# A fused attention and gMLP kernel: its order of all steps made anew, k's maxima in three steps, part of the layer-norm statistics on ScalarE

## The chip, the cores and the metric

The kernel runs on one core of one Trainium2 chip. Its engines run side by side, each with a queue of its own that it works off in order: TensorE does matrix products into PSUM, VectorE, ScalarE and GpSimd do elementwise work, and SyncE issues the transfers between the chip's memory and SBUF. The profile calls them PE (PEld for the loading of its weights), DVE, ACT, POOL and SP. The metric is the device time in microseconds (us), the median of several runs.

## The reference

For 8 batches and 8 heads with 576 positions of 64 channels, q is normalised by a softmax over its channels, k by a softmax over the positions; each head's 64x64 matrix `kv` and then its output come from products with these. The heads side by side are the 512 channels of `x`, which goes through a gated MLP:

```python
q_s = exp(q - max(q, axis=-1));  q_s /= sum(q_s, axis=-1) + 1e-09
k_s = exp(k - max(k, axis=2));   k_s /= sum(k_s, axis=2) + 1e-09
kv = einsum('bhsd,bhse->bhde', k_s, v)
x = einsum('bhsd,bhde->bhse', q_s, kv)      # heads side by side: (8, 576, 512)
h = gelu_tanh(x @ w_in)                     # (8, 576, 1024)
u, v = h[..., :512], h[..., 512:]
v_n = (v - mean(v)) / sqrt(var(v) + 1e-06) * g_ln      # over the 512 channels
v_s = einsum('ts,bsd->btd', w_sg, v_n) + b_sg[None, :, None]
out = x + (u * v_s) @ w_out
```

## The kernel before

**Sets and halves.** A batch is called a set, b = 0 to 7. q, k and v of a set come in two halves of four heads. SBUF has two buffers for each half-set of q, k, v, so SyncE (`Y`) fetches ahead.

**Precision.** fp32 values go through TensorE in a shorter fp32 form (fp32r): a value is split into a high part (a copy, which rounds) and a low part (value minus high part), and a product is made of three matmuls, high x high, low x high and high x low. Names that end in `_h` and `_l` (`wi`, `ws`, `wo` for w_in, w_sg, w_out; `x`; `vnh`, `vnl`; `gh`, `ulow`) are such parts. w_in and w_out arrive as 64-bit numbers and are turned into fp32 on the chip, a slice of 128 columns at a time (8 slices of w_in): `wi_a` scales the upper word on ScalarE, `wi_b`, `wi_c`, `wi_d` are a shift and two bit operations on VectorE that write tile `ot_i`, `wi_h` copies the high part on ScalarE, and `wi_l` subtracts for the low part, on GpSimd or, where the step says V, on VectorE. `wo_a` to `wo_l` do this for w_out with tile `ot_o`.

**The stages of a set.** k: `k_max` takes the maxima over positions (three VectorE instructions on tile `km`, 512, 256 and 256 wide), `kt_mm` transposes on TensorE, `k_top` finishes the maxima (`kt`), `kb_mm` spreads them over the partitions, `k_sub` and `k_exp` follow. q: `q_max` (tile `qm`), `q_swapm`, `q_top` and `q_sub`, `q_exp`, then `q_sum` (`qd`), `q_swapd`, `q_inv`, `q_mul` for the division and `q_turn` for the transposes. `kv_mm`, `kv_inv`, `kv_scale` give kv (tile `kvt`), `x_mm` gives x in four tiles, and `x_high`, `x_low` split it. Then `hv_mm` makes a 128-position tile of v (four per set, and a fifth for the two 64-position remainders of two sets, 36 in all), `hv_gelu` its gelu on ScalarE, `hv_stat` its mean and variance on VectorE with the two batch-norm instructions and one that adds 1e-06 (`ve`), `hv_pow` the power -1/2 on GpSimd (`rs`), `hv_norm`, `hv_high`, `hv_low` the normalised tile and its parts; `tail_high`, `tail_low`, `tail_again` do this for the remainders. `hu_mm` and `hu_gelu` give u, `sg_mm` the spatial product with w_sg, `gate`, `gate_high`, `gate_low` the gating, `out_mm`, `out_add`, `out_rest`, `out_store` the end. The last tile of set 7 is added, completed and stored in two halves (`last_mm`, `last_add`, `last_rest`, `last_store`).

**PSUM.** Three pairs of banks (`ps2`) go round for x, u, the spatial and the output products; two single banks (`ps1`) go round for k's transposes, kv and `hv_mm`. A new product waits until the bank that it is given has been read.

**What sets the order.** The string `PLAN` lists 1160 steps. They are issued one after the other as listed; the wrapper `InOrder` (its inner function `issue`, line 142) ties each instruction of VectorE, ScalarE, GpSimd and SyncE to the one issued before it on the same engine, and `mm` (line 330) keeps TensorE in program order. So the order of the steps in `PLAN` is the order of every engine's queue, and the position of a step against those of other engines sets nothing by itself. Line 142 therefore stands for all elementwise work in the profile, and tile names tell the work apart. A letter behind a step (`wi_l 1 V`) chooses its engine.

## Time and profile before

| what | value |
|---|---|
| median of 3 runs | 533.68 us (532.89 to 534.45) |
| the profiled execution: time, span on the core | 533.9 us, 532.0 us |
| busy in the span: PE, PEld | 484.2 us (91%), 444.3 us (84%) |
| busy in the span: DVE, ACT, POOL | 378.7 us (71%), 249.5 us (47%), 126.1 us (24%) |
| matmuls | 3824 |
| bytes read, written in the chip's memory | 38.83 MB, 9.44 MB |
| granted TensorE clock | 1.000 |

The span runs from the first to the last instruction of one profiled execution. Busy time is the time in which an engine had an instruction running; the profile's rows give an instruction's start and duration, or a group's busy time with its mean in ns, then the idle time just ahead of the group with what ended it. The span in 40 slices of 13.3 us shows PE nearly idle in the first four slices and full in nearly all others, DVE nearly full in the first ten.

### The profile page before, as it was taken

The page shows a single profiled execution, that of the slowest core. Times are in us where ns is not written, and L with a number is a line of the kernel's source. Part 1 is how long each engine was busy: PE and PEld are TensorE (multiplying, and loading weights), DVE is VectorE, ACT ScalarE, POOL GpSimd, SP SyncE. Part 2 cuts the span into 40 slices and gives each one's busy share as a digit, 9 for nine tenths or more (in the row PEclk, how much of TensorE's full clock was granted, in tenths as well). Part 3 has the DMA queues.
Part 4 walks back from the last instruction along what each step waited for, and adds up shares of the span by engine and source line. Part 5 has one row for each costly group of instructions (what it writes and reads, how often), then busy time and mean ns, then how long its engine had stood idle before and what let it go on. Part 6 is the DMA issues. An engine that isn't in the chain of part 4 may idle for free.

```text
span 532.0 us, 9264 instructions
## 1 busy us (share of the span) xinstructions
PE 484.2 (91%) x3824; PEld 444.3 (84%) x3824; DVE 378.7 (71%) x646; ACT 249.5 (47%) x425; POOL 126.1 (24%) x104
## 2 busy tenths in 40 slices
PE   0151999999999999999999999999999999999997
PEld 0040878998998988999999988999989988999997
DVE  8999899999879788876757887966264467243114
ACT  4474784658475355762564355751064134131110
POOL 0334403341332003251211322540111102012211
PEclk9999999999999999999999999999999999999999
...
GB/s 322 369 388 96 17 217 81 1 46 121 168 90 38 253 91 2 44 101 68 130 39 101 111 123 90 1 101 123 67 1 1 68 23 0 1 1 68 23 1 90
DMA packets 19054, 48.87 MB, mean 92 GB/s; under 512 B 1602, under 2 KB 8132, under 8 KB 19012
## 3 DMA queue, kind: packets, MB, share of 16 engines
...
HBM read 38.83 MB, written 9.44 MB: 91 GB/s over the span
## 4 chain that ended last, share of the span: by engine, by line
PE 74%; DVE 17%; issue 3%; DMA 2%; ACT 2%; POOL 1%; SPq 0%; POOLq 0%; DVEq 0%; ACTq 0%
PE ps L330 74%; DVE km L142 2%; DVE ot_i L142 2%; DMA qq<-q 1%; DVE qm L142 1%; DVE qd L142 1%; DVE kk L142 1%; DVE v L142 1%; POOL qq L142 1%; DMA kk<-k 1%; DVE qq L142 1%; DVE s L142 1%; DVE x_l L142 1%; DVE wi_l L142 1%; DVE ulow L142 1%
## 5 line engine op out<-in xcount | busy, mean ns | idle before, releaser
L142 POOL TENSOR_TENSOR rs<-ve,half 128x1 f32<-128x1 f32 x36 | 31.0, 860 | 157.1 <-DVE ve L142 152.1
L142 DVE TENSOR_TENSOR u<-ps,u 128x576 f32<-128x576 f32 x32 | 24.0, 750 | 52.0 <-PE ps L330 52.0
L330 PE MATMUL ps<-ulow,wo_h 128*128 128x288 f32 x256 | 55.7, 296 | 1.2 <-DVE ulow L142 1.2
L330 PE MATMUL ps<-gh,wo_h 128*128 128x288 f32 x256 | 56.1, 298 | 0.5 <-ACT gh L142 0.5
L330 PE MATMUL ps<-ws_h,vnh 128*128 128x288 f32 x256 | 55.8, 299 | 0.0
L330 PE MATMUL ps<-gh,wo_l 128*128 128x288 f32 x256 | 55.3, 294 | 0.0
L330 PE MATMUL ps<-ws_l,vnh 128*128 128x288 f32 x256 | 54.8, 295 | 0.0
L330 PE MATMUL ps<-ws_h,vnl 128*128 128x288 f32 x256 | 54.8, 295 | 0.0
L142 ACT ACT_TABLE_LOAD x38 | 48.8, 1283 | 8.0 <-PE ps L330 5.1
L142 ACT ACTIVATE v<-ps 128x512 f32<-128x512 f32 x36 | 21.5, 598 | 63.8 <-PE ps L330 62.3
L142 ACT CAST gh<-u 128x576 fp32r<-128x576 f32 x32 | 21.5, 671 | 57.5 <-DVE u L142 57.3
L142 DVE TENSOR_TENSOR o<-ps,x_h 128x576 f32<-128x576 f32 (+1 forms) x33 | 24.2, 734 | 31.8 <-PE ps L330 31.8
L142 POOL TENSOR_TENSOR qq<-qq,qd 128x576 f32<-128x576 f32 x22 | 28.2, 1295 | 68.6 <-DVE qd L142 46.2
L330 PEld LDWEIGHTS ps<-gh,wo_h 128*128 128x128 f32 x256 | 41.4, 188 | 1.9 <-ACT gh L142 0.8
L142 POOL TENSOR_TENSOR ulow<-u,gh 128x576 fp32r<-128x576 f32 x16 | 23.8, 1487 | 80.7 <-ACT gh L142 62.9
L330 PEld LDWEIGHTS ps<-ulow,wo_h 128*128 128x128 f32 x256 | 41.2, 188 | 2.0 <-DVE ulow L142 1.9
L330 PEld LDWEIGHTS ps<-ws_h,vnh 128*128 128x128 f32 x256 | 41.3, 189 | 0.4
L330 PE MATMUL ps<-wi_h,x_h 128*128 128x512 f32 x144 | 40.7, 404 | 1.0 <-DVE kk L142 1.0
L330 PEld LDWEIGHTS ps<-ws_h,vnl 128*128 128x128 f32 x256 | 41.3, 188 | 0.0
L330 PEld LDWEIGHTS ps<-ws_l,vnh 128*128 128x128 f32 x256 | 41.3, 188 | 0.0
L330 PEld LDWEIGHTS ps<-gh,wo_l 128*128 128x128 f32 x256 | 41.2, 188 | 0.0
L330 PE MATMUL ps<-x_h,wi_h 128*128 128x288 f32 x256 | 40.8, 303 | 0.0
...
## 6 DMA issues: line engine op xcount, KB each, us to landing
vv<-v SPq DMA_DIRECT2D x16, 650.0 KB, 6.1
...
qq<-q SPq DMA_DIRECT2D x16, 576.0 KB, 3.8
...
```

The lines of the kernel that those rows point to most:

```text
L142: ins = op(*args, **kw)
L330: tc.keep_in_program_order(nc.tensor.matmul(*args, **kw))
```

## The change

`PLAN` is replaced as a whole: 1217 steps in another order. Three things beside the order differ.

- `k_max` becomes three steps, `k_ma`, `k_mb`, `k_mc`, one instruction each, the same three instructions as before; other steps may stand between them.
- For 25 of the 36 tiles of v the mean and variance come from ScalarE: `hv_gelu … A` also writes the sum of its output (`sm`), the new step `hv_sq` scales it to minus the mean (`nm`) and squares the tile with that bias into a scratch tile `sq`, with the sum in `sv`; `hv_stat … A` is then one VectorE instruction on a 128x1 tile, and `hv_norm` adds `nm` in place of subtracting the mean.
- Engine letters differ: of the eight `wi_l` six run on GpSimd and two on VectorE (before two and six), of the five `ws_l` three run on VectorE (four before), `gate_low` is on GpSimd 11 times (16), `q_sub` on VectorE 10 times (8), `out_rest` on VectorE 19 times (20), and the first half's `last_rest` is on GpSimd.

Counted over the program, VectorE has 593 instructions in place of 641, ScalarE 369 in place of 331 with 26 table loads among them in place of 38, GpSimd 102 in place of 103, TensorE as many as before. SyncE's queue begins with slices 2 and 0 of w_in, the identity and slice 3 of w_in; q and k come behind them.

```diff
 PLAN = """
-load_q 0 1, load_q 0 0, load_k 0 1, load_k 0 0, load_eye, load_w_in 1, load_w_in 7, load_w_in 0, load_w_in 2, q_max 0 1, load_v 0 1, load_v 0 0
...
+load_w_in 2, wi_a 2, wi_b 2, wi_c 2, load_w_in 0, load_eye, load_w_in 3, load_q 0 1, load_k 0 0, load_w_in 1, load_q 0 0, load_k 0 1, load_b
+load_w_in 7, wi_a 0, wi_d 2, load_w_sg 0, wi_b 0, wi_c 0, wi_d 0, load_w_sg 1, load_w_in 4, wi_h 2, wi_a 3, load_v 0 0, load_v 0 1, load_w_sg 3
...
 """
...
@@ -200,6 +204,8 @@
     qq_s = slots("qq", 2, [P, 2, 18, 32])
     km_s = slots("km", 2, [P, 512])
     kt_s = slots("kt", 2, [P, 2])
+    sq = sb("sq", [P, DV])
+    sm_s, nm_s, sv_s = (slots(n, 6, [P, 1]) for n in ("sm", "nm", "sv"))
     qm_s, qs_s, qd_s, qe_s = (slots(n, 2, [P, 36]) for n in ("qm", "qs", "qd", "qe"))
     kr_s = slots("kr", 2, [P, 2])
     kvt_s, qt_s = slots("kvt", 2, [P, 2, D]), slots("qt", 4, [P, S])
@@ -339,12 +345,18 @@
     def load_v(b, h):
         Y.dma_start(out=vv_s(b, h, at=h), in_=v[b, h])
 
-    def k_max(b, h, E=V):
-
-        kk, m = kk_s(b, h, at=h), km_s(b, h, at=2 * b + h)
-        E.tensor_tensor(out=m, in0=kk[:, 0:2].rearrange("p t c -> p (t c)"), in1=kk[:, 2:4].rearrange("p t c -> p (t c)"), op=ALU.max)
-        E.tensor_tensor(out=m[:, 0:256], in0=m[:, 0:256], in1=m[:, 256:512], op=ALU.max)
-        E.tensor_tensor(out=m[:, 0:256], in0=m[:, 0:256], in1=kk[:, 4], op=ALU.max)
+    def k_ma(b, h):
+
+        kk = kk_s(b, h, at=h)
+        V.tensor_tensor(out=km_s(b, h, at=2 * b + h), in0=kk[:, 0:2].rearrange("p t c -> p (t c)"), in1=kk[:, 2:4].rearrange("p t c -> p (t c)"), op=ALU.max)
+
+    def k_mb(b, h):
+        m = km_s(b, h)
+        V.tensor_tensor(out=m[:, 0:256], in0=m[:, 0:256], in1=m[:, 256:512], op=ALU.max)
+
+    def k_mc(b, h):
+        m = km_s(b, h)
+        V.tensor_tensor(out=m[:, 0:256], in0=m[:, 0:256], in1=kk_s(b, h)[:, 4], op=ALU.max)
 
     def columns(ps):
         return ps[:, 0:256].rearrange("p (a n) -> p a n", a=2)
@@ -486,14 +498,26 @@
                 mm(ph, lhs(b)[:, c, col:col + P], rhs[:, c, DV:2 * DV], start=m == 0, stop=m == 11)
                 m += 1
 
-    def hv_gelu(b, i):
-        A.activation(v_s(b, i), st["hv", b, i], AF.Gelu_apprx_tanh)
-
-    def hv_stat(b, i):
-        s6, mv = s6_s(b, i), mv_s(b, i)
-        V.bn_stats(out=s6, in_=v_s(b, i))
-        V.bn_aggr(out=mv, in_=s6)
-        V.tensor_scalar(out=ve_s(b, i), in0=mv[:, 1:2], scalar1=1e-6, scalar2=None, op0=ALU.add)
+    def hv_gelu(b, i, E=V):
+        if E is A:
+            sm_s.take(b, i), nm_s.take(b, i), sv_s.take(b, i)
+            A.activation(v_s(b, i), st["hv", b, i], AF.Gelu_apprx_tanh, accum_out=sm_s(b, i))
+        else:
+            A.activation(v_s(b, i), st["hv", b, i], AF.Gelu_apprx_tanh)
+
+    def hv_sq(b, i):
+
+        A.mul(nm_s(b, i), sm_s(b, i), -1.0 / DV)
+        A.activation(sq, v_s(b, i), AF.Square, bias=nm_s(b, i), accum_out=sv_s(b, i))
+
+    def hv_stat(b, i, E=V):
+        if E is A:
+            V.tensor_scalar(out=ve_s(b, i), in0=sv_s(b, i), scalar1=1.0 / DV, scalar2=1e-6, op0=ALU.mult, op1=ALU.add)
+        else:
+            s6, mv = s6_s(b, i), mv_s(b, i)
+            V.bn_stats(out=s6, in_=v_s(b, i))
+            V.bn_aggr(out=mv, in_=s6)
+            V.tensor_scalar(out=ve_s(b, i), in0=mv[:, 1:2], scalar1=1e-6, scalar2=None, op0=ALU.add)
 
     def hv_pow(b, i):
         G.tensor_tensor(out=rs_s(b, i), in0=ve_s(b, i), in1=half, op=ALU.pow)
@@ -501,7 +525,8 @@
     def hv_norm(b, i):
 
         t = v_s(b, i)
-        V.scalar_tensor_tensor(out=t, in0=t, scalar=mv_s(b, i)[:, 0:1], in1=g_bc, op0=ALU.subtract, op1=ALU.mult)
+        mean, op = (nm_s(b, i), ALU.add) if (b, i) in nm_s.turn else (mv_s(b, i)[:, 0:1], ALU.subtract)
+        V.scalar_tensor_tensor(out=t, in0=t, scalar=mean, in1=g_bc, op0=op, op1=ALU.mult)
 
     def hv_high(b, i):
         A.activation(vn_hl()[0][:, i], v_s(b, i), AF.Copy, scale=rs_s(b, i))
```

Three places of the engines' queues follow. The first is VectorE from the scaling of set 0's second kv (`kvt0_1`) through the last of set 0's four `x_l` or as far as eleven rows reach; `ot_i` and `wi_l` are the conversion of w_in, `km1`, `qm1` the maxima of set 1. Before:

```order
L142 TENSOR_TENSOR kvt0_1_329<-ps1_1_77,kr0_1_317 128x128
L142 TENSOR_REDUCE qm1_1_331<-qq1_1_221 128x36
L142 TENSOR_TENSOR x_l0_340<-ps2_1_74,x_h0_325 128x576
L142 TENSOR_TENSOR qm1_0_323<-qm1_0_323,qs1_0_333 128x36
L142 SCALAR_TENSOR_TENSOR ot_i_4_273<-raw_wo_h_85,ot_i_4_273 128x512
L142 TENSOR_TENSOR km1_0_350<-kk1_0_256 128x512
L142 TENSOR_TENSOR km1_0_350<-km1_0_350 128x256
L142 TENSOR_TENSOR km1_0_350<-km1_0_350,kk1_0_256 128x256
L142 TENSOR_TENSOR qm1_1_331<-qm1_1_331,qs1_1_342 128x36
L142 TENSOR_TENSOR wi_l_62<-ot_i_4_273,wi_h_61 128x4x128
L142 TENSOR_TENSOR wi_l_62<-ot_i_2_175,wi_h_61 128x4x128
```

And now:

```order
L146 TENSOR_TENSOR kvt0_1_322<-ps1_1_78,kr0_1_317 128x128
L146 TENSOR_TENSOR x_l0_329<-ps2_0_74,x_h0_315 128x576
L146 TENSOR_REDUCE qm1_0_333<-qq1_0_270 128x36
L146 TENSOR_TENSOR x_l0_329<-ps2_1_75,x_h0_315 128x576
L146 SCALAR_TENSOR_TENSOR ot_i_6_264<-raw_wo_l_87,ot_i_6_264 128x512
L146 SCALAR_TENSOR_TENSOR ot_i_7_175<-raw_wo_l_87,ot_i_7_175 128x512
L146 TENSOR_TENSOR qm1_0_333<-qm1_0_333,qs1_0_349 128x36
L146 TENSOR_TENSOR km1_0_285<-km1_0_285,kk1_0_246 128x256
L146 TENSOR_TENSOR km1_1_359<-kk1_1_312 128x512
L146 TENSOR_REDUCE qm1_1_365<-qq1_1_310 128x36
L146 TENSOR_TENSOR x_l0_329<-ps2_0_74,x_h0_315 128x576
L146 TENSOR_TENSOR x_l0_329<-ps2_2_76,x_h0_315 128x576
```

Before, one `x_l` stands in this stretch, and the other three come behind it; now all four stand in it, and the two `wi_l` are gone from it.

The second place is GpSimd's queue from its first piece of work, with `qq` the products of q and `ws_2` the low parts of the bias. Before:

```order
L142 TENSOR_TENSOR qq0_0_93<-qq0_0_93,qd0_0_165 128x576
L142 TENSOR_TENSOR qq0_1_91<-qq0_1_91,qd0_1_152 128x576 x2
L142 TENSOR_TENSOR ws_2_66<-vb_0_89,ws_2_66 1x320
L142 TENSOR_TENSOR ws_2_66<-vb_1_90,ws_2_66 1x320
L142 TENSOR_TENSOR wi_l_62<-ot_i_3_206,wi_h_61 128x4x128
L142 TENSOR_TENSOR wi_l_62<-ot_i_7_267,wi_h_61 128x4x128
L142 TENSOR_TENSOR ws_l_64<-ghws_3_150,ws_h_63 128x640
L142 TENSOR_TENSOR qq1_0_191<-qq1_0_191,qm1_0_323 128x1152
L142 TENSOR_TENSOR qq1_1_221<-qq1_1_221,qm1_1_331 128x1152
L142 TENSOR_TENSOR qq1_0_191<-qq1_0_191,qd1_0_381 128x576 x2
```

And now:

```order
L146 TENSOR_TENSOR wi_l_62<-ot_i_2_93,wi_h_61 128x4x128
L146 TENSOR_TENSOR wi_l_62<-ot_i_3_124,wi_h_61 128x4x128
L146 TENSOR_TENSOR wi_l_62<-ot_i_1_152,wi_h_61 128x4x128
L146 TENSOR_TENSOR ws_l_64<-ghws_0_115,ws_h_63 128x640
L146 TENSOR_TENSOR qq0_0_105<-qq0_0_105,qd0_0_190 128x576 x2
L146 TENSOR_TENSOR qq0_1_100<-qq0_1_100,qd0_1_210 128x576 x2
L146 TENSOR_TENSOR wi_l_62<-ot_i_4_198,wi_h_61 128x4x128
L146 TENSOR_TENSOR wi_l_62<-ot_i_5_266,wi_h_61 128x4x128
L146 TENSOR_TENSOR qq1_0_270<-qq1_0_270,qm1_0_333 128x1152
L146 TENSOR_TENSOR qq1_1_310<-qq1_1_310,qm1_1_365 128x1152
```

Three `wi_l` now open the queue and two more stand ahead of set 1's q; before there were two in this stretch, behind q of set 0 and the bias.

The third place is ScalarE around the first statistics of v, with `u0` and `v0` the gelus of set 0 and `kk1` the exponentials of k of set 1. Before:

```order
L142 ACTIVATE v0_3_475<-ps1_1_77 128x512
L142 COPY qe1_1_480<-qd1_1_445 32x36 x4
L142 ACTIVATE u0_1_500<-ps2_2_75 128x576
L142 ACT_TABLE_LOAD
L142 ACTIVATE kk1_0_256<-kk1_0_256 128x1280
L142 ACT_TABLE_LOAD
L142 ACTIVATE v0_1_534<-ps1_1_77 128x512
L142 ACT_TABLE_LOAD
L142 ACTIVATE kk1_1_313<-kk1_1_313 128x1280
```

And now:

```order
L146 ACTIVATE u0_2_523<-ps2_2_76 128x576
L146 ACTIVATE u0_1_525<-ps2_1_75 128x576
L146 ACTIVATE v0_3_527,sm0_3_528<-ps1_0_77 128x512
L146 COPY qe1_1_530<-qd1_1_476 32x36 x4
L146 ACTIVATE nm0_3_535<-sm0_3_528 128x1
L146 ACTIVATE sq_73,sv0_3_537<-v0_3_527,nm0_3_535 128x512
L146 ACT_TABLE_LOAD
L146 ACTIVATE kk1_1_312<-kk1_1_312 128x1280
L146 ACT_TABLE_LOAD
L146 ACTIVATE v0_1_590,sm0_1_591<-ps1_0_77 128x512
```

The gelu of tile 3 now also writes `sm`, and the scaling to `nm` and the square with its sum stand between that gelu and k's exponentials.

More of the change, by code (lines that the diff above doesn't have):

```diff
@@ new lines @@
+x_high 0 1, q_max 1 0, x_mm 0 1, load_w_out 3, wi_l 5, ws_h 2, load_v 1 0, x_low 0 1, q_swapm 1 0, wi_c 6, wi_d 7, wi_h 7, q_top 1 0, k_mc 1 0
+k_ma 1 1, kt_mm 1 0, x_high 0 2, x_high 0 3, q_max 1 1, q_sub 1 0, q_swapm 1 1, wo_a 1, x_low 0 3, x_low 0 2, hu_mm 0 1, k_mb 1 1, k_top 1 0, k_mc 1 1
+q_top 1 1, q_exp 1 0, wo_a 0, ws_h 1, kb_mm 1 0, kt_mm 1 1, hu_mm 0 2, wi_l 7 V, wi_d 6, wi_h 6, k_sub 1 0, q_sub 1 1, k_top 1 1, k_exp 1 0, q_sum 1 0
+wi_l 6, kb_mm 1 1, hv_mm 0 3, q_exp 1 1, k_sub 1 1, b_l, wo_a 3, q_swapd 1 0, wo_a 2, q_sum 1 1, kv_mm 1 0, hu_mm 0 0, wo_b 1, hu_gelu 0 2
```

189 lines of the change are left out of this document (94 added, 95 removed).

## The prediction

> **What bounds the kernel now.** I read the split of the span by stage first, cutting it where the PE timeline changes character: 4 us (first data on DVE), 54 us (first dense matmul), 97 us (first spatial matmul), 168 us, 515 us. Columns: stage, its length, then busy us (and instructions) of PE, PEld, DVE, ACT, POOL.
>
> ```profile
> 4.00:54.00 50.00, 12.90 (x121) 7.78 (x121) 48.10 (x76) 27.73 (x57) 15.32 (x10) 1.00 0.83 296
> 54.00:97.00 43.00, 41.72 (x308) 35.30 (x309) 39.87 (x79) 30.13 (x53) 11.07 (x11) 1.00 0.30 97
> 97.00:168.00 71.00, 69.50 (x567) 66.52 (x566) 63.12 (x100) 44.85 (x78) 23.22 (x17) 1.00 0.24 80
> 168.00:515.00 347.00, 347.00 (x2736) 322.07 (x2737) 218.30 (x378) 144.83 (x238) 74.89 (x61) 1.00 0.18 64
> ```
>
> From 168 to 515 us PE never pauses, so there nothing but the number of matmuls counts, and the change keeps that number. All that can be won lies ahead of 168 us. In the first 50 us DVE is busy for 48.1 us and PE for 12.9; from 54 to 97 us DVE still has only 3.1 us free. Next, PE's waits, for 54 to 168 us and then for 168 us to the end:
>
> ```profile
> PE ps L330 <- DVE ulow L142: 1.0, 2, 0.7
> PE ps L330 <- DVE kk L142: 1.0, 1, 1.0
> PE ps L330 <- ACT gh L142: 0.5, 1, 0.5
> PE ps L330 <- DVE kt L142: 0.3, 1, 0.3
> ...
> PE ps L330 <- DVE ulow L142: 0.5, 2, 0.3
> ```
>
> 2.8 us and 0.5 us. So the time is: when the dense run of matmuls begins, plus a nearly fixed length, plus the tail. What starts it is in the PE timeline:
>
> ```profile
> 53.86 2.29 PE L330 MATMUL ps<-x_h,wi_h 128*128 128x288 f32 x8
> ...
> 58.73 1.18 PE L330 MATMUL ps<-wi_h,x_h 128*128 128x512 f32 x4
> ...
> 61.62 1.23 PE L330 MATMUL ps<-x_h,wi_h 128*128 128x288 f32 x8
> ...
> 96.23 0.43 PE L330 MATMUL ps<-ws_h,vnh 128*128 128x288 f32 x2
> ```
>
> The chain of waits ahead of 53.86 us is DVE work piece after piece: the weights' conversion (ot_i, wi_l), k's maxima (km), q's sums, then x_l. **DVE's queue up to the fourth x_l, and up to the last vn of set 0, sets when PE becomes dense.**
>
> **The change, part by part.** The rows that price it are DVE's groups from 4 to 54 us, then from 54 to 97 us (busy us, mean ns, idle before):
>
> ```profile
> L142 DVE TENSOR_TENSOR wi_l<-ot_i,wi_h 128x512 fp32r<-128x512 f32 x5 | 5.3, 1069 | 0.0
> L142 DVE TENSOR_REDUCE qd<-qq 128x36 f32<-128x1152 f32 x3 | 4.0, 1344 | 0.0
> L142 DVE TENSOR_SCALAR ot_i<-ot_i 128x512 uint32<-128x512 uint32 x8 | 3.3, 420 | 0.0
> L142 DVE TENSOR_TENSOR km<-km,kk 128x256 f32<-128x256 f32 x4 | 1.7, 426 | 0.1
> L142 DVE TENSOR_TENSOR qq<-qq,qd 128x576 f32<-128x576 f32 x1 | 0.8, 758 | 0.0
> ...
> L142 DVE BATCH_NORM_STATS2 s<-v 128x6 f32<-128x512 f32 x5 | 3.4, 679 | 0.1
> L142 DVE BATCH_NORM_AGGREGATE mv<-s 128x2 f32<-128x6 f32 x5 | 0.9, 182 | 0.2
> L142 DVE TENSOR_SCALAR ve<-mv 128x1 f32<-128x1 f32 x5 | 0.8, 154 | 0.2
> ```
>
> *Work ahead of the fourth x_l.* Counting both orders' DVE rows up to it, the new one has four wi_l fewer (they go to POOL), one qd, one shift of ot_i (ot_o), two of k's 256-wide maxima, one combination of q's maxima (36 wide, taken as 0.2) and one q product: 4 x 0.684 (a wi_l that nothing blocks, in the row further down) + 1.34 + 0.42 + 2 x 0.43 + 0.2 + 0.76 = 6.3 us less.
>
> *Work ahead of the first spatial matmul* (through tail_low of set 0): the same four wi_l (2.7), five pairs of BATCH_NORM (5 x 0.861 = 4.3) and one maximum (0.4) fewer; one q product (0.8), one such combination (0.2) and one ve (0.15) more; a ws product of 64 rows is replaced by one of like cost. Net 6.3 us again. So the gain at the start is not eaten by work put off to the next 43 us. **First term: -6.3.**
>
> *What POOL's help costs.* Five wi_l now run on POOL ahead of the fourth x_l (tiles 2, 3, 1, 4, 5), before two. The trace shows DVE stopped by POOL: at 42 us a maximum of k waits out a POOL product.
>
> ```profile
> 42.06 2.62 DVE L142 TENSOR_TENSOR km<-kk 128x512 f32<-128x512 f32 x1
> ...
> 41.62 2.51 POOL L142 TENSOR_TENSOR qq<-qq,qm 128x1152 f32<-128x1152 f32 x1 [1.20 <-DVE qm L142]
> ...
> L142 DVE TENSOR_TENSOR km<-kk x4: 649/678/2616, 8.4 to 49.1; 128x512 f32<-128x512 f32 x4
> ...
> L142 DVE TENSOR_TENSOR wi_l<-ot_i,wi_h x6: 681/684/2616, 15.7 to 57.3; 128x512 fp32r<-128x512 f32 x6
> L142 POOL TENSOR_TENSOR wi_l<-ot_i,wi_h x2: 1270/1436/1603, 30.7 to 37.3; 128x512 fp32r<-128x512 f32 x2
> ```
>
> Usually 678 ns, here 2616: 1.9 us lost, and the same once for wi_l. A reduction is not stopped:
>
> ```profile
> 117.59 1.34 DVE L142 TENSOR_REDUCE qm<-qq 128x36 f32<-128x1152 f32 x1
> ...
> 117.75 2.13 POOL L142 TENSOR_TENSOR qq<-qq,qm 128x1152 f32<-128x1152 f32 x1 [0.44 <-DVE qm L142]
> ```
>
> Bounds for the five: 0, and 5 x 1.27 = 6.35. In the new order wi_l 2 becomes ready among the conversions of tile 0, wi_l 3 behind q_sub with a wi_l of DVE next, wi_l 4 among k's maxima; wi_l 1 stands beside a sum of q and k's subtraction, wi_l 5 beside a maximum of q and x_l. Three meet products, 3.8 us; part of the first two is absorbed where DVE waits for the first k-v product anyway (about 0.7 us idle by my walk down the queue), and a blocked DVE queue lets the next POOL piece catch up. **I take +2.5.** The Trainium skill (SBUF — State Buffer, "SBUF: two separate sides") calls the port pair of VectorE and GpSimd an exclusive lock: a VectorE instruction with two SBUF inputs, or in a two-port mode, and a GpSimd instruction keep each other out for the whole instruction. By that rule, with which the 2616 ns agree, the three cost 3.8 and the sum below would end at 530.4.
>
> *The loads.* SP now issues w_in 2, w_in 0, eye and w_in 3 ahead of q and k, and DVE's first work is a weight conversion behind an ACT scaling:
>
> ```profile
> 2.96 0.48 DVE L142 MEMSET vn<- 1x512 f32 x1
> 4.23 2.74 DVE L142 TENSOR_REDUCE qm<-qq 128x36 f32<-128x1152 f32 x2 [0.78 <-DMA qq<-q]
> ...
> 11.07 0.66 ACT L142 ACTIVATE ot_i<-raw_vnh 128x512 f32<-128x512 f32 x1 [1.41 <-DMA raw_vnh<-w_in]
> ...
> GB/s 322 369 388 96 17 217 81 1 46 121 168 90 38 253 91 2 44 101 68 130 39 101 111 123 90 1 101 123 67 1 1 68 23 0 1 1 68 23 1 90
> ...
> vv<-v SPq DMA_DIRECT2D x16, 650.0 KB, 6.1
> ...
> qq<-q SPq DMA_DIRECT2D x16, 576.0 KB, 3.8
> ```
>
> q landed at 4.2 us when it was first. A weight slice of 512 KB instead of 576, first in the queue, should land about then, and the ACT scaling adds 0.66: **+0.7.** Bounds: 0 (DVE had memsets until 3.4 us) and 6.8 (it lands at 11.07 as the sixth did). Behind it DVE has conversions of three tiles while q and k arrive. Through the second v the new queue carries six weight slices, two q, two k, two v, two pieces of w_sg (320 KB) and eye, 7.5 MB; at the page's first two slices (322 and 369 GB/s, 13.3 us each) that has landed by 22 to 23 us, and k's and v's product comes near 28 us in my walk. So the loads hide; if that cover is gone, the wait is what v is late.
>
> *Statistics on ACT.* Each of the 25 tiles adds a 128x1 scaling and a 128x512 Square with a sum; the nearest rows (all of the page's groups) are a 32x36 copy and vnh:
>
> ```profile
> L142 ACT COPY qe<-qd 32x36 f32<-32x36 f32 x64 | 14.0, 219 | 6.4 <-DVE qd L142 5.5
> L142 ACT ACTIVATE vnh<-v,rs 128x512 fp32r<-128x512 f32 x32 | 22.7, 720 | 26.5 <-POOL rs L142 14.5 <-DVE v L142 11.8
> L142 ACT ACT_TABLE_LOAD x38 | 48.8, 1283 | 8.0 <-PE ps L330 5.1 <-DVE kr L142 1.6 <-PEq L644 0.7
> ```
>
> 25 x 0.94 = 23.5 us more; the order has 26 table loads instead of 38, 15.4 us less. Net 8.1 us on an ACT that is busy 30 of 43 and 45 of 71 us in the two middle stages: hidden by PE, and 8.1 us if that cover is gone. The sum output of gelu is not in the trace: bounds 0 and one more 219 ns each (5.5 us), also under ACT's idle time; I take 0. On DVE 25 x 0.861 = 21.5 us go; what of it lies behind 168 us, where PE waits for no one, is worth nothing.
>
> *The middle.* With DVE ahead of PE sooner, PE's waits of 54 to 168 us should shrink. Bounds -2.8 and, for new waits in an order whose every row has moved, +2.8 (the same kind again). From the first spatial matmul to the end of set 0's fourth spatial product the old order has about 17 us of DVE work (its rows times their means) beside 18 us of PE's, the new one about 9: the next DVE work is no longer just in time. **-1.7.** k's maxima as three steps cost nothing by themselves: the same three instructions. Behind 168 us: bounds 0 and +2; I take 0. The tail (last add, rest, store) keeps its length; one half's rest goes to POOL, ahead of the last half.
>
> Sum: -6.3 + 2.5 + 0.7 - 1.7 = -4.8. The profiled execution took 533.9 us (span 532.0, 1.9 us around it), 0.2 over the median of 533.68. 533.9 - 4.8 = **529.1 us**.
>
> **The rivals.**
>
> 1. *POOL takes back what it took over.* All five wi_l block (6.35) and the start is 0.7 late: 7.05 against 6.3, so no earlier start; with the middle's -1.0, 533.9 + 0.7 - 1.0 = 533.6. For it: the 2616 ns. Against it: the other eight of POOL's ten pieces in the first stage stopped nobody by as much.
>
> 2. *Nothing blocks and the middle closes.* -6.3 and all 2.8 us of waits: 533.9 - 9.1 = 524.8. For it: DVE is the only engine that is full ahead of 97 us. Against it: a POOL that works more there.
>
> 3. *Slower: ACT hands banks back late.* hv products have two PSUM banks, freed by gelu, and ACT runs in order. In the vnh row ACT waits 14.5 us for POOL's rs (seven times, 3.9 us the longest). A gelu queued behind such a wait and a Square (3.9 + 0.94) passes the cover of one hv product (58.73 to 61.62 us, 2.9) by 1.9. Once in each of sets 2 to 7 that is 11.4 us: 533.9 - 4.8 + 11.4 = 540.5. It decides from the fourth such place on (over 6.4 us, past +0.3%). Against it: PE waited for no gelu in 347 us, with ACT at 42%.
>
> **How the numbers follow.** Differences under 0.3% (1.6 us) cannot be told from none here, so faster means under 532.1 and slower over 535.3. Forecast 0.52 (its own range 526 to 532); rival 2 0.20; rival 1, with a late first load, 0.17, of which a quarter ends under 532.1; rival 3 0.11. Faster 0.52 + 0.20 + 0.04 = 0.76, same 0.13, slower 0.11. The range reaches from rival 2 to past rival 1: 524 to 534.5.
>
> **What would show it.** First term: the first dense matmul near 50.5 us (53.86 - 3.1) and the first spatial one near 93 us. Blocking: wi_l rows of POOL before 54 us, and DVE rows of 1.9 us and more beside them; their excess is the +2.5. Loads: DVE's first row at 4.9 us. Middle: PE's waits between the dense start and 168 us at 1 us or so. ACT: squares near 0.72 us and no PE wait for gelu. The forecast is wrong if the first dense matmul is no earlier than 53 us, or if PE shows waits behind 168 us of more than 2 us.

## The result, and the profile after

The changed kernel takes 521.82 us (median of 4 runs, 521.68 to 522.66) against 533.85 us before (532.89 to 534.45): 0.978 of it, with a 95% interval of 0.9762 to 0.9798. That is 12.0 us less; forecast were 4.8 less. The direction was right, and the size was not: 521.8 lies below the whole range of 524.0 to 534.5.

The profiled execution has a span of 520.0 us, 12.0 below the 532.0 of before. In it VectorE has 596 instructions in place of 646, ScalarE 513 in place of 425 (50 of them are the readings of sums described further down), and GpSimd 104 as before; so VectorE has 50 fewer, not 48 as counted in the description of the change, and GpSimd has none fewer. Its stages are cut where those of before were cut (columns as there: stage, length, busy us and instructions of PE, PEld, DVE, ACT, POOL).

```profile
4.00:54.00 50.00, 20.97 (x178) 16.83 (x179) 47.04 (x77) 30.42 (x61) 21.51 (x15) 0.93 0.86 305
54.00:97.00 43.00, 43.00 (x322) 36.50 (x321) 39.06 (x74) 36.78 (x82) 14.88 (x14) 1.00 0.24 90
97.00:168.00 71.00, 71.00 (x650) 67.74 (x649) 59.07 (x93) 38.25 (x75) 19.67 (x16) 1.00 0.38 124
168.00:515.00 347.00, 347.00 (x2679) 323.02 (x2678) 204.92 (x347) 150.26 (x297) 65.25 (x57) 1.00 0.16 56
```

From 54 to 515 us PE is now busy all the time. The chain of waits says the same: from 44.39 us to the end of the last matmul, 471.02 us, it is one stretch of PE.

```profile
44.39 471.02 PE ps L336 x3704
```

PE's waits from 36 us on, in the changed kernel, are two, and both lie ahead of that stretch:

```profile
PE ps L336 <- DVE km L146: 2.4, 1, 2.4
PE ps L336 <- DVE kvt L146: 2.2, 1, 2.2
```

The PE timeline of the changed kernel gives the same places that were quoted of before: the first matmul with w_in, the first spatial one, and the last.

```profile
44.73 2.27 PE L336 MATMUL ps<-x_h,wi_h 128*128 128x288 f32 x8
...
85.67 0.51 PE L336 MATMUL ps<-ws_h,vnh 128*128 128x288 f32 x2
...
515.10 0.29 PE L336 MATMUL ps<-gh,wo_l 128*128 128x288 f32 x1
```

Two cuts of PE's time, from the first matmul with w_in to the first spatial one and from there to the end of the last matmul, hold the whole account. Before:

```profile
53.86:96.23 42.37, 41.09 (x305) 34.67 (x304) 39.25 (x78) 29.41 (x51) 11.07 (x11) 1.00 0.30 99
96.23:528.33 432.10, 430.39 (x3403) 402.02 (x3401) 288.44 (x487) 191.10 (x318) 99.53 (x79) 1.00 0.19 66
```

After:

```profile
44.73:85.67 40.94, 40.94 (x302) 34.93 (x301) 39.28 (x73) 34.78 (x78) 16.23 (x13) 0.95 0.41 152
85.67:515.39 429.72, 429.72 (x3405) 401.70 (x3403) 272.12 (x452) 198.09 (x388) 90.92 (x77) 1.00 0.19 66
```

The two stretches hold nearly the same numbers of matmuls in both kernels. So the 12.0 us are: the dense run begins 9.1 earlier (53.86 to 44.73); PE's idle time behind that, 42.37 - 41.09 = 1.3 and 432.10 - 430.39 = 1.7, is gone, 3.0; its busy time is 0.8 less (0.15 and 0.67); and from the end of the last matmul to the end of the span it takes 0.9 more (520.0 - 515.39 = 4.6 in place of 532.0 - 528.33 = 3.7). -9.1 - 3.0 - 0.8 + 0.9 = -12.0.

### The profile page after: what moved, and what is told of

It reads as the page before. It is cut to its first block, busy times and chain, and to the rows that moved or that the text cites. A ratio compares the mean times of both kernels' runs of the same rounds, so it can differ in the third digit from the quotient of the medians.

```text
span 520.0 us, 9276 instructions
## 1 busy us (share of the span) xinstructions
PE 482.4 (93%) x3824; PEld 444.2 (85%) x3824; DVE 353.8 (68%) x596; ACT 257.0 (49%) x513; POOL 122.3 (24%) x104
## 4 chain that ended last, share of the span: by engine, by line
PE 92%; DVE 5%; DMA 2%; ACT 1%; issue 0%; SPq 0%
PE ps L336 92%; DVE ot_i L146 2%; DMA kk<-k 1%; DMA raw_vnl<-w_in 1%; DVE km L146 1%; DVE qm L146 1%; DVE qq L146 0%; DVE qd L146 0%; DVE o L146 0%; DVE qt L146 0%; DVE kk L146 0%; ACT ot_i L146 0%; ACT kk L146 0%; ACT qe L146 0%; DVE wi_l L146 0%
## 5 line engine op out<-in xcount | busy, mean ns | idle before, releaser
L146 POOL TENSOR_TENSOR rs<-ve,half 128x1 f32<-128x1 f32 x36 | 26.3, 736 | 132.3 <-DVE ve L146 115.7
L336 PE MATMUL ps<-gh,wo_l 128*128 128x288 f32 x256 | 55.4, 295 | 0.0
L146 ACT ACTIVATE u<-ps 128x576 f32<-128x576 f32 x32 | 20.7, 651 | 46.4 <-PE ps L336 46.2
L146 POOL TENSOR_TENSOR qq<-qq,qd 128x576 f32<-128x576 f32 x22 | 29.5, 1355 | 46.7 <-DVE qd L146 25.2
L336 PE MATMUL ps<-x_h,wi_l 128*128 128x288 f32 x256 | 40.0, 299 | 0.0
```

The costliest lines, as they stand in the source:

```text
L146: ins = op(*args, **kw)
L336: tc.keep_in_program_order(nc.tensor.matmul(*args, **kw))
```

## The experiments

Each kernel was timed against the kernel before on the same chip. The table puts their traces into the same account: start of the dense run (first matmul with w_in), PE's idle and busy time from there to the last matmul, first spatial matmul, in us; ratio with its 95% interval.

| kernel | median | ratio to before | start | idle | busy | first spatial |
|---|---|---|---|---|---|---|
| before | 533.85 | 1 | 53.86 | 3.0 | 471.5 | 96.23 |
| changed | 521.82 | 0.978 (0.9762 to 0.9798) | 44.73 | 0.0 | 470.7 | 85.67 |
| e1 start only | 535.11 | 1.0013 (1.0001 to 1.0025) | 44.98 | 11.3 | 473.9 | 98.04 |
| e2 rest only | 531.68 | 0.9948 (0.9931 to 0.9965) | 55.82 | 0.0 | 469.4 | 95.18 |
| e9 to the first spatial matmul | 530.80 | 0.9927 (0.9909 to 0.9945) | 45.67 | 6.5 | 473.6 | 86.78 |
| e3 w_in's low parts on VectorE | 523.97 | 0.9803 (0.9786 to 0.982) | 46.25 | 0.0 | 471.4 | 87.86 |
| e12 three of them | 521.74 | 0.9779 (0.9748 to 0.981) | 44.55 | 1.7 | 471.8 | 88.25 |
| e4 statistics on VectorE | 528.77 | 0.9895 (0.9875 to 0.9916) | 45.13 | 4.0 | 473.4 | 90.77 |
| e10 only early statistics on ScalarE | 524.12 | 0.9807 (0.9792 to 0.9821) | 45.23 | 1.4 | 471.2 | 86.03 |
| e5 before, statistics on ScalarE | 533.73 | 0.9985 (0.9975 to 0.9994) | 54.34 | 2.3 | 471.9 | 97.31 |
| e8 before, q_sub on VectorE | 530.46 | 0.9923 (0.9907 to 0.9938) | 50.41 | 2.7 | 471.9 | 93.26 |
| e15 before, both of e5 and e8 | 529.62 | 0.9913 (0.9897 to 0.993) | 50.28 | 2.5 | 471.3 | 92.72 |
| e11 before, x_l forward | 533.26 | 0.9986 (0.9974 to 0.9999) | 44.46 | 8.4 | 475.0 | 95.31 |
| e17 e15, x_l and slice 6 forward | 533.06 | 0.9984 (0.9974 to 0.9993) | 44.44 | 7.7 | 474.7 | 95.39 |
| e13 order before, engines after | 541.67 | 1.0137 (1.0113 to 1.0161) | 57.37 | 4.9 | 472.6 | 102.08 |
| e14 order after, engines before | 532.96 | 0.998 (0.9966 to 0.9994) | 46.88 | 4.2 | 475.1 | 92.92 |
| e7 first product of u forward | 525.55 | 0.9845 (0.9821 to 0.9869) | 43.24 | 3.1 | 472.6 | 89.12 |
| e19 q_sub on VectorE | 524.12 | 0.9816 (0.9801 to 0.9831) | 44.96 | 1.6 | 471.1 | 87.91 |
| e6 tail, second half moved | 522.48 | 0.9782 (0.9764 to 0.9801) | 45.11 | 0.6 | 471.3 | 86.39 |
| e16 tail in the order before | 521.37 | 0.9762 (0.9742 to 0.9782) | 45.16 | 0.7 | 471.7 | 86.82 |

In these groups of runs the kernel before had medians of 533.85 to 534.51 us, and each ratio's interval reaches about 1 us to either side. Between two kernels of the table that are both changed, a difference of less than some 1.5 us is therefore not told from none, and the starts of the dense run differ by up to 0.5 us where nothing ahead of them was edited (changed, e4, e6, e10, e16).

The first four asked which part of the change the gain belongs to.

**e1, the start alone.**

```diff
-(the plan of the kernel before up to its first hu_mm, 161 steps)
+(the first 150 steps of the new plan, up to its first hu_mm)
 (all other steps in the order before, statistics on VectorE)
```

> Only the start of the new order: its steps up to the first matmul with w_in, then all other steps in the order of the kernel before, statistics all on VectorE. Theory 1 (what starts the dense run is VectorE's queue up to x's low parts, and that queue alone is what the new start changes): first dense matmul at 44.7 us as in the changed kernel (53.86 before), waits behind it as before (3.3 us), so 533.9 - 9.1 = 524.8. Rival (the new start only puts VectorE's work off, and the stages behind it pay): the dense run starts at 44.7 too, but PE's waits grow by the work put off, about 4 us, so 529.

The dense run began at 44.98, and nothing was gained: 0.7 us slower by the ratio (0.0013 x 534). PE's waits in e1, and its timeline at the longest of them:

```profile
PE ps L334 <- ACT wi_h L144: 8.1, 1, 8.1
...
58.53 2.08 PE L334 MATMUL ps<-wi_h,x_h 128*128 128x512 f32 x4 [8.09 <-ACT wi_h L144]
```

The first hv product needs slice 6 of w_in, whose conversion now stands behind the work that the start had put off (the maxima of k, which GpSimd stops, GpSimd's second subtraction, and a sum of q that waits 3.2 us for ScalarE; ScalarE itself had stood 4.5 us until a slice of w_out landed). The rival is right here, and by more than it said. My theory 1 falls: when the dense run begins is not enough.

**e2, the rest alone.**

```diff
 (the first 161 steps of the plan before)
-(all other steps in the order before)
+(all other steps in the new order, statistics of 25 tiles on ScalarE)
```

> Only the rest of the new order: the steps of the kernel before up to its first matmul with w_in, then the new order with its statistics on ScalarE. Theory 1 (start and rest are separate gains): dense run from 53.9 us as before, PE's 3.3 us of waits behind it gone, tail 0.9 longer as in the changed kernel: 533.9 - 3.3 + 0.9 = 531.5. Rival (the waits vanish only because everything ahead starts earlier): waits stay at 3 us, 534.8.

531.68: PE's idle time behind the start is gone entirely, as theory 1 had it, the tail is 4.6, and the start stays late (55.82, even 2.0 later than before). By the ratios, e1's 0.7 slower and e2's 2.8 faster do not add up to 12.0 faster.

**e3, GpSimd's low parts of w_in back on VectorE.**

```diff
-wi_l 1, wi_l 2, wi_l 3, wi_l 4, wi_l 5, wi_l 6
+wi_l 1 V, wi_l 2 V, wi_l 3 V, wi_l 4 V, wi_l 5 V, wi_l 6 V
```

> The changed kernel with the six low parts of w_in that GpSimd makes given back to VectorE. Theory 1 (what GpSimd takes over it takes back by stopping VectorE): four of them lie ahead of the second x_l, and a fifth just ahead of it, 5 x 0.68 = 3.4 us more on VectorE, and the three stops of 3.1 us beside them are gone: within 0.7 us of 521.8, dense run from about 45 us. Rival (GpSimd's help is most of the gain at the start): 3.4 later, 525.2.

2.2 us slower than the changed kernel by the medians, 1.2 by the ratios, whose intervals just overlap. The trace lies between the two: the dense run begins 1.5 later, neither 0 nor 3.4, so the stops beside GpSimd's pieces give back about half of what it takes over, not all.

**e4, the statistics back on VectorE.**

```diff
-hv_gelu b i A, hv_sq b i, hv_stat b i A    (25 tiles)
+hv_gelu b i, hv_stat b i
```

> The changed kernel with the layer-norm statistics of all 36 tiles on VectorE. Theory 1 (the start is not touched, and VectorE has only 2.4 us free from 42.7 to 88 us, where five pairs of batch-norm instructions, 4.3 us, come back): dense run from 44.4 us, waits of up to 1.9 us come back ahead of the first spatial matmul, 521.8 to 523.7. Rival (statistics on ScalarE are what closed PE's waits): the 3.3 us of waits return in full or more, 525 and above.

7.0 slower (6.1 by the ratios): the rival. The dense run begins where it did; the first spatial matmul comes 5.1 later, with 2.8 us of PE waiting again, and behind it 1.1 us of waits come back. PE's busy time grows by 2.7; part of this is that its matmuls run slower behind the longest wait, 1.9 us at 81.5 (its clock is 0.50 from 82.2 to 85.6; see the last section).

The next four asked where the statistics and the stops act.

**e5, the order before with statistics on ScalarE.**

```diff
-hv_gelu b i, hv_stat b i
+hv_gelu b i A, hv_sq b i, ..., hv_stat b i A    (25 tiles)
```

> The order before, with the statistics of the same 25 tiles on ScalarE (the square right behind its gelu). Theory 2 (two limits in series: when the dense run can begin, and whether VectorE keeps up with it until the first spatial matmul): VectorE has 4.3 us less ahead of the first spatial matmul, but the dense run still begins at 53.9 us, and PE has only its waits to lose, 2.3 us ahead of the first spatial matmul and 1.7 behind: 534.2 less 2.5 to 4, about 531. Rival (statistics on ScalarE are worth what giving them back cost the changed kernel, 7 us, whatever the order): 527. Second rival (ScalarE hands hv's banks back late): 534 and above.

0.8 faster, not 2.5 and not 7. VectorE's waits over the whole of e5 say why:

```profile
DVE ve L146 <- ACT sq L146: 31.1, 20, 4.0
```

In the order before, the instruction that finishes the variance stands so close behind the gelu that VectorE stands still for the square, 31 us in 20 places, 4.1 of them in 4 places ahead of the first spatial matmul. In the changed kernel the same wait is

```profile
DVE ve L146 <- ACT sq L146: 5.0, 4, 2.4
```

because the new order has other steps between; ahead of its first spatial matmul it is 0.5 in one place. So in e5 VectorE's 4.3 us less of work ahead of the first spatial matmul became idle time on it.

**e8, two subtractions of q taken from GpSimd, in the order before.**

```diff
-q_sub 1 0, ..., q_sub 1 1
+q_sub 1 0 V, ..., q_sub 1 1 V
```

> The kernel before with the two subtractions of set 1's q, which stop VectorE for 1.9 us each at 42 and 46 us, on VectorE itself, in their place behind the second x_l. The dense run should begin 3.8 earlier, at 50.0, since both stops lie ahead of the second x_l; the 2 x 1.36 of the subtractions come behind it. Theory 2: by the first spatial matmul only 3.8 - 2.7 = 1.1 is left, 533.1. Rival (the beginning of the dense run decides alone): 530.4.

4.0 faster with two letters. VectorE in e8, where the kernel before had its 2.62 and 3.22 us (for one maximum and two wi_l):

```profile
42.47 0.69 DVE L144 TENSOR_TENSOR km<-kk 128x512 f32<-128x512 f32 x1
...
44.09 1.29 DVE L144 TENSOR_TENSOR wi_l<-ot_i,wi_h 128x512 fp32r<-128x512 f32 x2
...
47.49 0.75 DVE L144 TENSOR_TENSOR x_l<-ps,x_h 128x576 fp32r<-128x576 f32 x1
48.16 2.62 DVE L144 TENSOR_TENSOR qq<-qq,qm 128x1152 f32<-128x1152 f32 x2
```

Both stops are gone, the second x_l comes at 47.5 in place of 50.9, and the dense run at 50.41, 3.4 earlier. The rival is right: the two subtractions that VectorE took over did not come back as waits.

**e9, the new order up to its first spatial matmul.**

```diff
 (the new plan up to its first sg_mm)
-(the rest of the new plan)
+(all other steps in the order before, statistics on VectorE)
```

> The new order through its first spatial matmul, with the statistics of its six tiles on ScalarE, then all other steps in the order before with statistics on VectorE. Theory 2 (all that is gained is gained ahead of the first spatial matmul): first spatial matmul at 85.7 us as in the changed kernel, behind it the order before with its waits of up to 1.7 us and its tail, 0.9 shorter: 521.8 + 1.7 - 0.9 = 522.6. Rival (the new start puts work off that the stages behind it pay, as when only the first 150 steps were taken): 526 and above.

The rival again: the first spatial matmul came at 86.78, and 6.5 us of waits behind it took most of that back. PE's waits in e9 from 36 to 180 us:

```profile
PE ps L334 <- DVE u L144: 3.1, 1, 3.1
PE ps L334 <- DVE vn L144: 2.4, 1, 2.4
```

**e10, only the early statistics on ScalarE.**

```diff
-hv_gelu b i A, hv_sq b i, hv_stat b i A    (25 tiles)
+hv_gelu b i A, hv_sq b i, hv_stat b i A    (6 tiles: set 0's five and one of set 1)
```

> The changed kernel with statistics on ScalarE for the six tiles ahead of the first spatial matmul alone, the other 19 back on VectorE. Theory 2: 521.8 to 522.5, as PE does not wait behind 86 us. Rival (the later ones count too: with all 36 on VectorE the time from the first spatial matmul to the last matmul was 2.0 longer): 523.8.

2.3 slower than the changed kernel by the medians (1.4 by the ratios, whose intervals just overlap). Of the 7.0 that the statistics are worth there, the six tiles ahead of the first spatial matmul bring about 4.7 and the other 19 about 2.3. The trace shows where: PE waits 0.4 us at 202.8 and 0.8 at 206.7, which the changed kernel does not. That PE hardly waited behind 168 us before did not make later VectorE work free.

Five more tried to improve on one of the two kernels.

**e6 and e16, the tail.** In the changed kernel the first half's add (`o<-ps,x_h`, 288 wide, both halves in the first of these rows) begins only when the second half's last matmul is over, and its two rests lie beside each other:

```profile
515.43 0.82 DVE L146 TENSOR_TENSOR o<-ps,x_h 128x288 f32<-128x288 f32 x2 [1.61 <-PE ps L336]
516.29 0.79 DVE L146 TENSOR_TENSOR o<-o,x_l 128x288 f32<-128x288 f32 x1
...
515.97 0.80 POOL L146 TENSOR_TENSOR o<-o,x_l 128x288 f32<-128x288 f32 x1 [4.61 <-DVE o L146]
```

```diff
 e6:
-last_mm 7 0, last_mm 7 1, out_add 7 0, ..., last_add 7 0, ..., last_rest 7 0 G
+last_mm 7 0, out_add 7 0, ..., last_add 7 0, last_mm 7 1, ..., last_rest 7 0 V
 e16: the last 20 steps as in the plan before
```

> The changed kernel with its last steps in another order: the second half of the last product is issued behind the add of the first half, and the first half's rest is on VectorE. In the changed kernel the first half's add begins at 515.43 us, with the last matmul of the second half just over, though its own matmuls ended at 513.6, and both rests run beside each other at 0.8 us in place of 0.46. Theory (the add waits for the last matmul issued ahead of it on the same PSUM tile): last matmul to end 3.7 us as before in place of 4.6, so 0.9 less, 520.9. Rival (the end is bound by the stores): no change, 521.8.

> The changed kernel with its last 20 steps in the order before, so that a whole product stands between the two halves of the last one: the first half's add is done before the second half's matmuls are issued, and they do not wait for it. Last matmul to end 3.7 us in place of 4.6, and no wait of PE of 0.6 as in the run where only the second half was moved: 520.9. Rival: the tail is not bound by these (no change, 521.8).

In both the last matmul is 3.7 us ahead of the end, as the theory said. In e6 the second half's matmuls then waited 0.6 for the first half's add on the same PSUM tile:

```profile
515.07 0.40 PE L336 MATMUL ps<-gh,wo_h 128*128 128x288 f32 x1 [0.55 <-DVE o L146]
```

In e16 that wait is gone; its trace shows 0.7 us of another, for an x_l, in the dense run. By the times, 522.48 and 521.37 against 521.82, neither can be told from the changed kernel; the dense run began 0.4 later in both profiled executions, which no step of theirs explains.

**e7, an earlier first product in the new order.**

```diff
+x_low 0 3, x_low 0 2, q_max 1 1, ..., hu_mm 0 1, kt_mm 1 0, k_mb 1 1
-kt_mm 1 0, ..., q_max 1 1, ..., x_low 0 3, x_low 0 2, hu_mm 0 1, k_mb 1 1
```

> The changed kernel with set 0's third and fourth x_l ahead of the maxima of q's second half on VectorE, and the transposes of set 1's k behind the first product of u on TensorE. Theory (the first product stands behind a transpose that waits 2.4 us for k's maxima; VectorE has room): dense run from 42.3 in place of 44.7 us, 519.5 to 521. Rival (VectorE is just in time behind it, and what starts earlier waits later): waits come back by the same amount, 521.8.

3.7 slower, worse than the rival: the start came 1.5 earlier, and 3.1 us of waits came behind it, with slower matmuls: 1.9 for the maxima of set 1's k, which the edit puts off, 0.9 for a high part of x on ScalarE and 0.3 for a transpose of q. The 2.4 us for which PE waits at 42 us in the changed kernel are not free to take.

**e12, the three stopped pieces back.**

```diff
-wi_l 2, wi_l 3, wi_l 4
+wi_l 2 V, wi_l 3 V, wi_l 4 V
```

> The changed kernel with three of GpSimd's six low parts of w_in (slices 2, 3 and 4) on VectorE, those beside which VectorE was stopped, 3.1 us in all. Theory (a piece given to GpSimd saves 0.68 us, and costs about 1 where it lands beside an instruction that it stops): 3.1 - 3 x 0.68 = 1.0 faster, 520.8, dense run from 43.7. Rival (each piece given back costs the same, as the 2.2 us for all six say): 0.36 x 3 = 1.1 slower, 522.9.

521.74 with 521.18 to 524.37 over four runs, the profiled one the longest of them: neither the 1.0 faster nor the 1.1 slower is shown.

**e11, in the order before only x's low parts moved.**

```diff
-x_low 0 1, ..., wi_l 4 V, wi_l 2 V, ..., x_low 0 0, ..., x_low 0 2, ..., x_low 0 3
+x_low 0 1, x_low 0 0, x_mm 0 1, ..., wi_l 4 V, wi_l 2 V, x_high 0 2, x_high 0 3, x_low 0 2, x_low 0 3
```

> The kernel before with only the low parts of set 0's x moved: the second directly behind the first (from 51 to 41.4 us), the third and fourth behind the low part of w_in's slice 2. No work leaves VectorE. Theory 3 (order alone: the second x_l frees the PSUM tile for x's last tiles, and what stands ahead of it sets the beginning): first matmul with w_in at 44 to 46 us, its third part waits for the fourth x_l at 51, 6 us earlier than before; behind it some 2 us of new waits for the conversion of w_in's slice 6: 534.4 - 4 = 530.4. Rival (VectorE's total work up to the fourth x_l decides, as the prediction had it): no more than the 1.5 us of maxima put off, 532.9.

The first matmul with w_in came at 44.46, as theory 3 said, without any work leaving VectorE; the time is nevertheless nearer the rival's 532.9. Hardly anything was gained all the same, 0.7 us, since that product and the next one then waited for the conversion of w_in. PE's waits in e11:

```profile
PE ps L334 <- DVE wi_l L144: 3.0, 1, 3.0
PE ps L334 <- ACT wi_h L144: 2.1, 1, 2.1
```

What was open then was whether order or engines carry the gain. The next two complete a square.

**e13, the order before with the new engines, and e14, the new order with the engines before.**

```diff
 e13: order before; wi_l 1 to 6, gate_low, q_sub, q_mul, out_rest, ... and 25 tiles' statistics as in the changed kernel
 e14: new order; all these, and the statistics, as in the kernel before
```

> The order before with every choice of engine as in the changed kernel (six low parts of w_in on GpSimd, statistics of 25 tiles on ScalarE, and the letters of 54 further steps). If the gain of 12 is the engines' (order only carries them): 522 to 525. If order and engines work only together: the statistics alone gave 0.8 in this order, the low parts of w_in take 3.4 from VectorE ahead of the second x_l, of which the stops by GpSimd give part back, so 530 to 532.

> The new order with every choice of engine as before, statistics on VectorE. If the gain is the order's: 523 to 526. If order and engines work only together: what giving back the low parts of w_in cost (2.2) and what giving back the statistics cost (7.0) add up, 521.8 + 9.2 = 531.

The engines alone are 7.5 us slower, the order alone 1.2 faster, both together 12.0 faster. For e13 none of my numbers was near. VectorE and GpSimd in e13 from 45 to 53 us show it:

```profile
45.89 1.37 DVE L146 TENSOR_TENSOR km<-km,kk 128x256 f32<-128x256 f32 x1
...
48.36 2.40 DVE L146 TENSOR_SCALAR ot_o<-ot_o 128x512 uint32<-128x512 uint32 x1
50.67 2.61 DVE L146 TENSOR_TENSOR km<-kk 128x512 f32<-128x512 f32 x1
...
45.71 2.66 POOL L146 TENSOR_TENSOR wi_l<-ot_i,wi_h 128x512 fp32r<-128x512 f32 x2 [7.76 <-ACT wi_h L146]
48.34 4.39 POOL L146 TENSOR_TENSOR qq<-qq,qm 128x1152 f32<-128x1152 f32 x2
```

Two wi_l moved to GpSimd stand there in a row with the two subtractions, and three instructions of VectorE that take 0.42, 0.42 and 0.68 us elsewhere (and a short one between them) are stopped one after the other. Summed over VectorE's rows up to the first spatial matmul, each counted as work up to the shortest of its kind in the three kernels and as a stop beyond it, e13 has 7.0 us less work than before and 5.7 more of stops. The changed kernel has 8.4 less work and only 0.5 more of stops.

**e15, both cures in the order before.**

```diff
-q_sub 1 0, ..., q_sub 1 1, ..., hv_gelu b i, hv_stat b i
+q_sub 1 0 V, ..., q_sub 1 1 V, ..., hv_gelu b i A, hv_sq b i, ..., hv_stat b i A
```

> The order before with set 1's two subtractions of q on VectorE (which gave 4.0 alone) and the statistics of the 25 tiles on ScalarE (0.8 alone). If the two are separate: 534 - 4.8 = 529.2. If statistics on ScalarE pay once the dense run begins earlier (VectorE was busy 50.4 of 52 us from 45 to 97 when it took the subtractions back): up to 4.3 more at the first spatial matmul, 525 to 527.

529.62 (4.6 faster by the ratio): the two are separate and add up, and the earlier start did not make the statistics pay. VectorE still waits 30 us for squares there.

**e17, all named limits cured in the order before.**

```diff
 (e15, and x_low, x_mm, x_high of set 0 moved as in e11)
+..., wi_l 2 V, wi_l 4 V, wi_a 6, x_high 0 2, x_high 0 3, x_low 0 2, x_low 0 3, wi_b 6, wi_c 6, wi_d 6, wi_h 6, ..., wi_l 6 V
```

> The order before with set 1's subtractions of q on VectorE, the statistics of the 25 tiles on ScalarE, set 0's low parts of x moved forward as in the earlier run, and the conversion of w_in's slice 6, for which that run waited, behind them. If the gain can be had by curing the named limits one by one: dense run from about 44 us, PE's waits behind it 2 us, 534.1 - 9 = 525. If each cure only uncovers the next late piece of VectorE's queue: 528 to 530, no better than the 529.6 without the move of x.

533.06, worse than e15 and than either expectation: with the start at 44.44, new waits appear at once. The two longest of PE's waits behind the start in e17:

```profile
PE ps L336 <- ACT v L146: 2.7, 1, 2.7
PE ps L336 <- DVE kt L146: 2.5, 1, 2.5
```

**e19, e8's edit in the new order.**

```diff
-q_sub 1 0, ..., q_sub 1 1
+q_sub 1 0 V, ..., q_sub 1 1 V
```

> The changed kernel with the same two subtractions on VectorE that gained 4.0 in the old order. If the stops belong to where a piece of GpSimd lands, and the new order has none beside these two (k's 512-wide maximum took 0.68 there, 2.62 before): nothing to win, and 2.7 us more on VectorE, 522 to 525. Rival (GpSimd's subtraction costs VectorE wherever it stands): 519.

2.3 slower (1.9 by the ratios), as the theory said: what gained 4.0 in the old order costs in the new one, where these subtractions stop nobody. VectorE and GpSimd in the changed kernel:

```profile
44.25 0.68 DVE L146 TENSOR_TENSOR km<-kk 128x512 f32<-128x512 f32 x1
44.85 1.34 DVE L146 TENSOR_REDUCE qm<-qq 128x36 f32<-128x1152 f32 x1
46.12 1.41 DVE L146 TENSOR_TENSOR x_l<-ps,x_h 128x576 fp32r<-128x576 f32 x2
...
44.13 2.79 POOL L146 TENSOR_TENSOR qq<-qq,qm 128x1152 f32<-128x1152 f32 x1 [2.22 <-DVE qm L146]
```

The new order has the subtraction run beside a reduction and two x_l, which are not lengthened; the maximum ahead of them takes its usual 0.68, and GpSimd's piece 2.79 in place of 2.51.

**What the runs say together.** The kernel has two limits in series: when the dense run begins, and whether VectorE has each later piece ready when PE comes to it, mostly ahead of 170 us and in part behind it (e10). Moving the first without the second gives 0.7 slower to 0.7 faster (e1, e11), the second without the first 2.8 faster (e2). In these runs GpSimd's help and ScalarE's statistics pay only where the order puts them beside work that they do not stop and far enough ahead of who waits for them (e13 against the changed kernel, e5 against e4). Which of the new order's moves are needed for it was not found: e17's few moves are not.

## Why the prediction was wrong, step by step

**"DVE's queue up to the fourth x_l ... sets when PE becomes dense": the wrong gate, and the step that failed first.** The fourth x_l ended at 47.5 us in place of 55.4, 7.9 earlier; the dense run began 9.1 earlier, and ahead of that x_l. In the kernel before, PE waited for the second x_l, which frees the PSUM tile that x's last tiles need. PE's row of before, and VectorE's, were there to be read:

```profile
51.75 2.18 PE L330 MATMUL ps<-qt,kvt 64*64 64x288 f32 x12 [10.96 <-DVE x_l L142]
...
50.94 0.75 DVE L142 TENSOR_TENSOR x_l<-ps,x_h 128x576 fp32r<-128x576 f32 x1
```

e11 shows that this x_l is the gate of the old order: with it moved forward (the two behind it too, though later than 44.5 us), the first matmul with w_in comes at 44.46.

The changed kernel has another gate. It has set 0's first two `x_low` in exchanged order, so that the first x_l in VectorE's queue frees that PSUM tile, at 40.8 us in place of 51.7, and x's last tiles are done at 42.0. (e3, in the new order, shows PE waiting 0.56 us for this first x_l.) What PE waits for then is a maximum of set 1's k, whose transpose stands ahead of the first product in TensorE's queue. PE in the changed kernel, then VectorE:

```profile
40.16 1.87 PE L336 MATMUL ps<-qt,kvt 64*64 64x288 f32 x16 [2.21 <-DVE kvt L146]
44.39 0.69 PE L336 MATMUL ps<-eye,km 128*128 128x128 f32 x2 [2.35 <-DVE km L146]
...
43.92 0.42 DVE L146 TENSOR_TENSOR km<-km,kk 128x256 f32<-128x256 f32 x1
```

So the 9.1 us have two parts. VectorE finishes what PE waits for 7.3 earlier (44.34 in place of 51.69). And from there PE needs 0.4 to its first matmul with w_in in place of 2.2, since x's last tiles no longer stand between: 1.8, which no term of the prediction has. It is the order's: e14, the new order with the engines before, has the same gate, a wait of 2.0 us for the maximum at 46.5.

*The 7.3 on VectorE.* Ahead of this maximum the new order has four wi_l, a reduction of q's maxima, one 512-wide and two 256-wide maxima of k, a q product, a shift for w_out and a 36-wide combination fewer than before ahead of the second x_l, and one two-input bit operation of w_in's conversion more: -6.3. That this is the number of the prediction is chance, as it is counted to another instruction from another list. The stops and the loads, below, give -0.7 and +0.6. About 0.9 more is what the prediction put at nothing, "k's maxima as three steps": in the kernel before, each 256-wide maximum begins 0.03 us behind the end of the maximum that it needs, eight times ahead of the gate, while in the new order, with other steps between, it begins 0.08 before the end of the row ahead of it. 8 x 0.11 = 0.9 is an estimate from these rows; no run changes the splitting alone. Together -7.3.

**"Three meet products, 3.8 us ... I take +2.5": the count was right, the sum was not.** Three stops stand ahead of the gate in the changed kernel, the shift, a maximum and a pair of bit operations beside GpSimd's wi_l. VectorE's rows, then GpSimd's:

```profile
7.10 2.36 DVE L146 SCALAR_TENSOR_TENSOR ot_i<-raw_vnh,ot_i 128x512 uint32<-128x512 uint32 x2
...
14.63 1.49 DVE L146 TENSOR_SCALAR ot_i<-ot_i 128x512 uint32<-128x512 uint32 x1
...
37.56 1.49 DVE L146 TENSOR_TENSOR km<-km 128x256 f32<-128x256 f32 x1
...
7.46 1.45 POOL L146 TENSOR_TENSOR wi_l<-ot_i,wi_h 128x512 fp32r<-128x512 f32 x1 [7.02 <-ACT wi_h L146]
13.97 1.87 POOL L146 TENSOR_TENSOR wi_l<-ot_i,wi_h 128x512 fp32r<-128x512 f32 x1 [5.06 <-ACT wi_h L146]
...
37.17 1.60 POOL L146 TENSOR_TENSOR wi_l<-ot_i,wi_h 128x512 fp32r<-128x512 f32 x1 [4.19 <-ACT wi_h L146]
```

They cost 2.36 - 1.42 = 0.9, 1.49 - 0.42 = 1.1 and 1.1: 3.1. But the two stops of before, 1.9 each, which I had quoted as the price of GpSimd's help, were part of the 53.86 and fell away. The sum charged the new ones and did not credit the old: the term is 3.1 - 3.8 = -0.7 in place of +2.5, the largest single error of the sum, 3.2. e8 shows what the old ones were worth in the old order, 4.0.

**The loads, +0.7: right.** VectorE's first row behind the memsets, now a conversion, began at 4.85 in place of 4.23. So for the start the prediction had -6.3 + 2.5 + 0.7 = -3.1, and the traces show -6.3 - 0.7 + 0.6 - 0.9 - 1.8 = -9.1.

**"The middle, -1.7": mis-sized.** All 3.0 us of PE's idle time went, and 0.8 of its busy time. It takes the statistics on ScalarE to close them (e4: 7.0 slower without). Of these I had the later ones as work that is "worth nothing" behind 168 us; e10, without them, is some 2 us slower and has its waits at 203 and 207 us.

**"Statistics on ACT": hidden, as said, but dearer.** From 36 us on no wait of PE in the changed kernel is for ScalarE. A tile costs ScalarE 1.31 us, not 0.94, since each sum has a reading of its own, which I had left at 0 for the gelu and not seen for the square. For 25 tiles that is 32.8 us, above even the bound of 23.5 + 5.5. ScalarE's busy time grew by 7.5 us all the same (257.0 against 249.5), near the 8.1 of the prediction, but by luck: the durations of its instructions together grew by 16.9, and more of them overlap. ScalarE's groups in the changed kernel:

```profile
L146 ACT ACTIVATE sq<-v,nm 128x512 f32<-128x512 f32 x25 | 18.1, 725 | 0.8
...
L146 ACT ACTIVATE nm<-sm 128x1 f32<-128x1 f32 x25 | 5.1, 203 | 0.5
...
L146 ACT ACTIVATION_READ_ACCUMULATOR v<-ps 128x1 f32 x25 | 4.9, 197 | 0.1
...
L146 ACT ACTIVATION_READ_ACCUMULATOR sq<-v,nm 128x1 f32 x25 | 4.7, 186 | 0.0
```

**"The tail keeps its length": wrong by 0.9.** The rows at e6 show two reasons, and without them the tail is 3.7 us again in both e6 and e16; the times of these two do not show a gain.

**The rivals.** Rival 2 (nothing blocks and the middle closes, 524.8) was right on the middle and nearest in the time, though stops do occur. But it took the start for 6.3 earlier with the stops at nothing, where 9.1 and a new gate were measured, so that its time was near is in part luck. Rival 1's mechanism is real and showed in e13, in the old order. Rival 3, ScalarE handing banks back late, did not happen in the changed kernel. A wait of PE for `v` on ScalarE of 0.8 us did in e4 and e10, behind a wait of ScalarE for VectorE, and one of 2.7 us in e17; in none of the three does a square stand just ahead of that gelu.
